# Conformer layer on one core: 56 of the 69 chunk transposes as DMA transposes

## The chip, the cores and the metric

The kernel runs on one core of a Trainium2 chip. A core has five engines, each with its own instruction stream: TensorE (PE, with the weight loads shown as PEld), VectorE (DVE), ScalarE (ACT), GpSimd (POOL) and SyncE (SP, which only issues DMAs here). The metric is device time of one execution in microseconds (us). Of three runs of the kernel before, the median is 881.56 us (881.25 to 883.18).

## The reference

Two sequences of 4000 tokens with 144 features in bf16 pass one conformer layer: half a feed-forward block, attention with 4 heads of 36, a gated convolution block, half a feed-forward block, and a layernorm. Each block works on a layernorm of x.

```python
h = _layernorm(x);  x = x + 0.5 * (_silu(h @ w_ff1a) @ w_ff1b)          # 144 -> 576 -> 144
h = _layernorm(x);  q, k, v = split(h @ w_qkv)                          # 4 heads of 36
att = softmax(q @ k.T * 36 ** -0.5) @ v;  x = x + att @ w_o             # 4000 x 4000 a head
h = _layernorm(x) @ w_pw1;  h = h[..., :144] * _sigmoid(h[..., 144:])
c = sum(hp[:, i:i + T, :] * dw[i] for i in range(5));  x = x + _silu(c) @ w_pw2
h = _layernorm(x);  x = x + 0.5 * (_silu(h @ w_ff2a) @ w_ff2b)
return _layernorm(x)
```

## The kernel before

**Tiles.** The tokens are cut into 16 chunks of 500 (`NCH`, 8 per sequence), and a chunk into 4 blocks of 125 tokens, which lie on the partitions; token p of a chunk's 500 is on partition p // 4. x stays in SBUF (`X`). A matmul wants the features on the partitions, so each layernorm output (`XN`, tokens on partitions) is transposed into `XT` (a chunk's 500 tokens in two parts, features 0 to 127 and the 16 that are left, padded to 80 rows) or, for q, k and v, into `XTQ` (two parts of 72 features). The attention output `AN` is transposed into `XT` in the same way, for W_o. That makes chunk transposes of four kinds in the middle of the kernel, 69 in all: 13 into `XTQ` and 56 into `XT`, 15 of these from `AN`. The first three chunks and the end of the kernel (`calm`, L975) transpose on PE.

**One chunk transpose** (`transp`, L1038, and `transp_q`, L1017, both by `blocks`, L994) goes through HBM. DVE transposes blocks of 32 x 32 words of four bytes in place, so two blocks of tokens are kept interleaved in pairs of bf16 (`XNI`, `ANI`, `XTJ`, `XTF` are views of that layout). SP then issues four DMAs that write the result into rows of a DRAM tensor (`rows`, `DR`), waits until they land, and issues two that read it back, transposed as a whole, into `XT` or `XTQ`. The matmuls that read `XT` (`xt`, L981) then step over the partner's elements, so their moving operand has a step of two elements. `XT`'s second part is zeroed once per slot by POOL (L1044), since the read fills only 16 of its 80 rows. `AN` is zeroed as a whole by POOL (L931, 128 x 2560) before its first use. There are 5 slots of `XN`, 5 of `XT` and 4 of `AN`.

**Layernorm** (`ln`, L1068): DVE makes the statistics, POOL the power -0.5 and the scaled row (`XN`), for chunks in the middle.

**Attention.** For each of 16 query chunks there are 63 tiles of keys of 64. PE makes the scores of a tile (two banks of PSUM), ACT the exponential (128 x 1000), and PE multiplies by v. Of these tiles 190 take another way: DVE makes the exponential by bit operations (`dve_tile`, L1770, five instructions each). All other blocks are woven in between: the front makes q, k and v of the 8 chunks of the first sequence; then attention runs over the query chunks, and the second sequence's first blocks, the convolution and the second feed-forward follow beside it.

**What sets the order.** The kernel is written as generators; a planner (`Sched`, L488, `pick`, L1899) gives each instruction a cost and a time and so makes a first order per engine. `Rec.op` (L177) records every instruction with what it reads and writes; all instructions are issued from one line, L398, which is therefore the line of nearly everything in the profile. Then `Rec.reorder` (L279) moves blocks of each engine's list by the letters of a table (`ORDER`, L38; P is "stay"), and `PLACES` (L111) gives the PSUM bank of each tile. Both tables were found by a search. `Rec.finish` (L344) puts the semaphore waits. The loads of x for the second sequence are issued by SP after a set number of chunk transposes (`later`, L860, in `blocks`).

The write and the read of one transpose, from `blocks`:

```python
op("dve", "transpose", v, v, r=[key], w=[key], cost=c_dve(320))
...
for a in range(4):
    args = "sp", "dma_start", DR[z, :, :, a, :, :].rearrange("k r g n -> r g k n"), v[32 * a:32 * a + 32, :, :, :]
...
for dst, f0, f1, n, cost, lat in reads:
    args = "sp", "dma_start", dst, d[f0:f1, :, :, :].rearrange("f g a n -> f g (a n)")[:, :, 0:n]
```

Of the kernel before, what the change touches and what calls it, by code (L numbers as in the profile page):

```python
# [8 lines left out]
F32 = mybir.dt.float32  # L9
# [30 lines left out]
        "PPPPPPQOQOPPPPPRPNPPQQQQLPPQORPNPRPTMORNNVO~OLNOMrMMNPMMNNNOMNNNOPLMQMMMNNPMMNSMNLMMOOPNSOMQMSPNOPU["  # L40
        "OMNRMOPPQIRMSNPNePNOOOcNNNNNNNNNOOLbNLOOQNSH]MMOLOMPMMOOOVPNOOOOPPPTOOOTPMUQMSLNNQQNQOQQNPPPPPTPPROK"
        "PPPPPPPPPPPP`PPPQKVPPKPPMPPRPUPPPROQQQRZOQQQRRKQRRSJPRRRRRRRWSZRNYUR~NHQ@R[KEGOOOPPPPKQOPPSPPSLPQMTP"
        "PPLQQQMPPPQVPPQOX_PTOPPCRTQQRGSQIQQSQRNV8OOQNNVSNOOLOPUUNN_MMWLNNRMMMMOOOPPPPPPQQNPPRSNRSSSORRVTR[OR"
        "AKQ@PPLOOQQNPPPPPUOOOOOPQOPPPPPUOOOOQRPLU`NNNXMMPNLQMNLZRNL`MN_YLLMK`KMNLILNQJMOOOPNYOPNOOOQNNZ^NNNN"
        "OOPNQNQOYP]CNNNNOMPMSO[NKOOQNVMPMMN`NbYMMMMNOMNIcLLNL[MMMNNQNRMJQLLROQSPLRNOQOPUQOMPQMPPRPVPLQOMQNPQ"
        "QQQSKPQSQKQQQQJPPPPPWQQSPKKQQUPPPSWPQRPQAVPPPQCVPQRPWHSYPHSOPQYPQEPQCPRZUPPSOOHDPR^OKOOOOPNOOOO^NOQN"
        "NOOOSNNNNS[NNNdRMNRKYNJWJNNNNNNGOOPP^YNNNNOMNNNNRNNPPPVROOLOOPPRZNNOOOOOPNOSOPNRPSMOOPQOQWNRPRLLNSZP"
        "NPQOIOQOTPPPRPQ]P^USPMMQIQKQQ8QTQQGMRRTQQKRRRRGLRSOMRPQQQJQQRPVP[OOOQEROO^IOQLNOOPPTTOMNQ[FOQNPPSPPM"
        "HPQOQQUPLOPNVPNOOSQNLUOOPNOXPPPLTQNLMPPPQOPPTOOPTPLOOQRNOPPPQOVPNOOOORZOP[PPMOOFRZOL[ROQKQTUBOKNFPPP"
        "_OOOOOOPNOOOOWNNVNNXMNTKMNOMZQOSLNOMSPSLLTPMOOUOPNOOTQOMOPPPQOPPPQOPPPTTQOSQSSSSNEEPQOPTPTMOMORSNNOP"  # L50
        "ROYPQOPQ^NPNPQOPAOOOOOSOOOPPPQQNPPPPPPXOOOOOOOaNPPPLOOOPUMOOOO[IOOPSOOQNPHPSWOOPPPPQGPPPPQQQMPPQQNPQ"
        "O_OOOPZOOOPI_NNNNZOPEOQWP^HKPHSJOLNOO`VPMRJOM^J`MPNKUNLUGNLJQNRIOPPRXOMOOOOPXMOPPMOOOPWOOPPPTKNOOPPP"
        "PPPPPPPQRPSYSQNQYZPRRRADIOXQGVOPJOORPIPPRRSSMR]MHOOQQQVRKNHPLPPPPPPPPPPRZQSQRRbHSGNQGPPQRRGLPQKQQQQJ"
        "QOQRPMQOPPQOSQNRMTROTNPXQQQEPJOQNPRPN_OPPPLRSOPLPPPGPPPSeOMPPQRJZPKLNNNN`NOKOVJNNNNcM`LMMMNNN]MNL]LL"
        "LLLLTWLXKMMVNQ_LMOPPQQ>MOOOTOMRbMMOOOOOTOOOQZIOPJMOOcOMPPT[PRORPEVHOPYCJQOQQGMOQQNQWNQNPPLSP_OaOOOPN"
        "PDPPPLOHPPQLPPPPQOTPNWNPPPWJNPPP`OIOPPPPPPPUQOELRP^TTQOZUPPCGOPQDJPPPPPPRPQWPRURPMFQQ_RPXDPQJLPNOJPN"
        "PPPPPSPPQ`PPTQQRERPQIQTNDPTPPJOPQQNPPUOPPSLPMPPRPQQRPJP[RNQQLaRJQSS[IQMGQQRPCZJPQOPQTPP@RPIPPPPQQQSS"
        "VXUQGNTQSSETDS`OQSCJQQdLOINQMRLLZMNSMMMMZLWPK]JMNLMTLNNNNVN`NNNNNROOPPJQOPLRPRMOQQRPLPXQQQRPTUQHFPQJ"
        "PPPPPPSPROUSPPTLPUOCOPNQOPROTWPRWRPVRZOY^YEOOPPMQ:;QDQQQQQQQQQEQQQMQOROVSMOTTQLVHROTRGNTVPHRPTRaJSQE"
        "QRSKNRNOQOPWQO=OOPNYOOOQNNOO]QOL_PNRO^NOUIPNK_MMW>MMMZMMMM]MMQLMMSNNOMOPPSOVNNPNXNPQOKQOQLQQQQUPPPHO"  # L60
        "QORPQMQOPQQSQOUVWNWMNOKOAOQOPPPPZWNNNOOLNNR^MNVNOMNNNNPSMN]NTNNNNNaNNNOQLN[RNOMRNHMSOSNPQGPQOPRXRPQW"
        "KOHOPPQYPPZPQRCO[I^NORFNNIZMMMNOWLNNNQMNRORRO_KPNOOOYNNNNNNOU^NSUHNKOJNOSOOQRJUPROTYMHNNURNNTMIPNQOU"
        "OOV[MNLNNNPYTNeJLNORNNGOO[]NNNNIQLMRLNRWOPUOO]OM`QO;LSOLO]JOJPRLLMRUNZMOVR[NPDOT^OOOFOSTOMNOSbPQLPRS"
        "_MORR_NPP^OHCNNNOZOWL~NHLMMNNNSOOXNOQQNSSOIVKPNPN]NOOOOOPPVOOOITNPPLPPQOWPPMRPNTKOOTNOPUMOOOQN`OOOPN"
        "OOPPPLOZOQQMPIQO^YROQQRLENO_PNPPPTQNNOROOSVO]QMNRNOPWTNOMNSOPQXbOOOQ[NO~NCdIMMMMMMMfbKMMMQMMJLMPLMUM"
        "MMNL^TR^JSLJQJUKPNLHQMPP`UNNNNOMOOOOPNOOPPPPQQNPQQQMUQQMSOPTQOPTPQUNQSPSQ<TRSSVEQQQHQQFPPPPPQSPMYTOL"
        "NNTMNNNP^[NOMNNQMMOLNN]PNOOR[OPKQN_ZLNESMOOKHOM[NPPLPNOOPPMQSTMNPQQQQRSQRRTCQVNGRNOMTTTMMNUPPQHNQSPM"
        "YVTQKLLSSOIJPSSPTMKORNOQOPPPPPPSORNSMRNRRRNQQRPFRPQQQQQQRPFQO"
# [14 lines left out]
    "dve": (
        "PPROQQQLPPPUUNNNNSMUNNPNOQOSPNSUMOPLOPTPNPNPPQQQQQQQQHPVPRPLPLPPPRSSNRNQVPUOODNUMPNPNPPQSPMXNOOQNNOO"
        "PPPPPPPSOOOPPQOPPPPPPPPPPPPPPPPQOQOPPPPPPROQQMQOQOPPQORSQMQQQQQRPQWQRPQLPQQQVQQQSUKTQ2KMPQQQRRORPQQR"
        "RRTQQRTTPP;RPQBPPSOOORPNSOPRPQKQOPPPPPPcPQcQQQQTPPERPDLDNRNRNQQQRFQNQQNQOPQOPPPQOPPPPPPPPPPPPPPPQQTM"
        "PPRPQQQQUQOQUQQQSQRVGPPPPSPPRPQQ/PQOPPSPPQQKPPPPPQOPPPPQOPPPPPROOPQQNROQNPPPPQOPQOQQNPPPQTQOPQRPSPRR"
        "NSPPRPQQQ;QOPPPPPPPPPPPROOQOPSOOOPQOROOUSUOOQSQHRGOPPPPROOPPQRPMQRNQNQOPPPPPPPPPPQOPRPRPQKQOPQQQRPQQ"
        "QQQWROOPQO?PPPPPPPPQOPSOPQePPROOPPEOPNOPNOOOOOQNPPPPPROOPPPPRPRRRRJQKPPQOPPPPPPPPPPPQOPPPYOOPNPRMSMR"
        "LQMPPQOPPPPPPPPPPPPPPPPPQOROOPROOPPPPPPPPQOPQOQOPPROOTOOOOQOSOOOPROQNPPPPPPPPPPPQSPPLQOPPPROOPPPPPPP"  # L90
        "PPPQOPPPPPPPPPPQOPPPPPQOPPPPPPPQQVPLTPMOLPPRPNPQOPPRRNNPROQNPPPPPPPPPPQOQOQORORNOPROOPPPQQNPPPPQOPQR"
        "NOPQOPPPPPSPNOQQNQOPQOPPPPPQQQMPPPPPPPQOPPPQOQRPMROQQMPPQOPSPNOPPUOOOOOWOOOOOOOPPQOPPQQQQRPRPQGPPPPP"
        "PPPPPPQOPPPPUOOOPNPQOSOOSNOSNZQMPLOPNOOOPPPPPPQQNQOQOPPPPQOQOPPPRUOUQOUIOJOOPPPQOPPPPUOOOOOPPPQOROQT"
        "QOPJQOPPPPPPPQQQMPQOPPQRNTNTNNNQNQOPQOROQNPPQOPPPPPPSPNOTOOOOPPPQOQQUPVQOTHPNIQOVOPPMPQMPTOPPRLTNOOO"
        "PPPPPPUOOOOOPQOPPSPSQSQSQUSTEOELQOPPPPPPPSOPNPPROOVOOPNOOPPROOVOOPNOOPQRPUQQQVRUQUPCKPDPPPPQOPPPPQOP"
        "QOQOSPNOhQOPPPPPHOPNOPPQOROQNGOOPPPQOQOPQOPRPNPPPPQOPPPPPROTPPLQRULVOUOJPNJPPQOQOPRPQMPPPPPPPPQQQQQK"
        "QRNRNORPNUOUP[LNKPMRNRNLNQSSMRMRPKQOQQNQOWPPMQOXOPRPNSOWNCPNORNRTTPJSQMSPPQRZOROQQQQTPUHOPRO4PPPPPPQ"
        "QQRLRPQLPPPPPPPPPQOQQQMPPPPPQQQMPPPPPPPPPQQQSLTRPSQJQQQQQRTOPPRPRSQSQRRTQUPQTDO/OPS]NSMOLNQQNLOVQUPU"
        "OKHPLRRNNPPPQOPQRPQQQQVQOPQORSOP?PPPPPPPPPPPPRORPQQRPWQQNPTPUPUKOO<OPQOROQQMPQOPQQNPQQSPTQNPHPPROOQS"
        "NPQULPNOORROQRPJPPSOOORO]SOSNPRWQQXPTRERGRRTTUXRTRSBSSSSSSSSAT@S&NNPPPPPPPPPPQO"  # L100
    ),
# [2004 lines left out]
```

## Time and profile before

| what | value |
|---|---|
| three runs: median (lowest to highest) | 881.56 us (881.25 to 883.18) |
| profiled execution: span from first to last instruction | 880.5 us |
| TensorE clock granted, mean | 0.998 |
| ACT, largest group: exponentials 128 x 1000 | 802, 749.3 us busy |
| DVE, largest group: PT from PS, 128 x 500 | 380, 250.1 us busy |
| DVE, chunk transposes (STREAM_TRANSPOSE) | 69, 34.5 us busy |
| POOL, XN rows 125 x 144 | 260, 150.4 us busy |
| POOL, memset of AN; memsets of XT | 1 of 2.23 us; 5 of 0.52 us |
| DMA queue q1 (SP's): packets, share of 16 engines | 112646, 13.8% |

The profiled execution has no time of its own besides its span; the median of the runs is 1.1 us above the span, and that is taken for what lies around it. Busy time of an engine is the union of its instructions' spans, and an instruction's span has a part that overlaps the next one, so a busy share near 100% can still hold small gaps. "Idle before" is the time an engine stood still ahead of a group, with what ended it. A row of the windows view gives the window, its length, then busy time and number of instructions for PE, PEld, DVE, ACT and POOL, then the granted clock, the DMA share and GB/s.

### The profile page before, as it was taken

Reading aid. Unit: us, or ns where it says so; the run is one execution under the profiler, and the core shown is the slowest. Engines: PE = TensorE matmul, PEld = TensorE weight load, DVE = VectorE, ACT = ScalarE, POOL = GpSimd, SP = SyncE. Lnnn points to the kernel's source line nnn. Section 1 sums busy time; section 2 is a strip of 40 time slices with the busy share of each in tenths; the row PEclk is TensorE's granted clock in tenths of the full one; section 3 lists DMA queues with packets and bytes.
Section 4 is the critical chain, followed back from the end, with each engine's and each line's share of the span. In section 5 each row is a group of like instructions: output and inputs, shape, how many; then the busy total and the mean of one; then the engine's idle time right before and its main releaser. Section 6 shows DMA issues by size and latency. Waiting matters only on the chain.

```text
span 880.5 us, 27000 instructions
## 1 busy us (share of the span) xinstructions
PE 851.5 (97%) x11419; PEld 380.2 (43%) x11419; DVE 822.7 (93%) x1812; ACT 849.6 (96%) x1098; POOL 300.4 (34%) x584
## 2 busy tenths in 40 slices
PE   8998999999999999999999999999999999999996
PEld 6543433344444443443444444344443433444366
DVE  7977999999999999999989999899999999999987
ACT  6799999999999999999999999999999999999986
POOL 7770331431336130252111813522513404032434
PEclk9999999999999999999999999999999999999999
DMA  3221001220221110212001120110110011001111
GB/s 100 44 55 38 16 18 36 62 51 16 40 49 38 23 38 22 45 24 45 16 9 30 36 44 23 23 26 20 43 31 18 21 37 20 17 12 36 27 27 33
DMA packets 114351, 28.80 MB, mean 33 GB/s; under 512 B 101090, under 2 KB 114230, under 8 KB 114230
## 3 DMA queue, kind: packets, MB, share of 16 engines
q1 hardware_dynamic: 112646, 26.39, 13.8%
q8 instruction: 89, 1.46, 0.7%
q10 hardware_dynamic: 1584, 0.69, 0.3%
q14 instruction: 32, 0.26, 0.1%
HBM read 13.44 MB, written 13.61 MB: 31 GB/s over the span
## 4 chain that ended last, share of the span: by engine, by line
ACT 46%; PE 33%; DVE 17%; POOL 2%; DMA 1%; issue 1%; SPq 1%; POOLq 0%; DVEq 0%
ACT PT L398 42%; PE PS L398 33%; DVE PT L398 7%; ACT TH L398 4%; DVE HT L398 2%; DVE ST L398 2%; DVE X L398 2%; DVE XN L398 2%; POOL RS L398 1%; POOL XN L398 1%; DVE KT L398 1%; DVE QT L398 1%; DVE AN L398 1%; SPq L398 1%; DMA rows<-XN 0%
## 5 line engine op out<-in xcount | busy, mean ns | idle before, releaser
L398 ACT ACTIVATE PT<-PS 128x1000 bf16<-128x1000 f32 (+1 forms) x818 | 757.2, 1074 | 4.1 <-PE PS L398 2.4
L398 PE MATMUL PS<-QT,KT 64*64 64x500 bf16 x3968 | 425.7, 385 | 13.0 <-ACT PT L398 5.2
L398 PE MATMUL PS<-PT,VA 64*37 64x500 bf16 x4728 | 411.5, 372 | 1.8 <-DVE QT L398 0.7
L398 DVE TENSOR_SCALAR PT<-PS 128x500 int16<-128x500 f32 x380 | 250.1, 668 | 5.8 <-PE PS L398 3.9
L398 PEld LDWEIGHTS PS<-QT,KT 64*64 64x64 bf16 x3968 | 123.4, 104 | 236.8 <-ACT PT L398 137.1
L398 POOL TENSOR_SCALAR RS<-ST 125x4 f32<-125x4 f32 x130 | 37.0, 284 | 482.2 <-DVE ST L398 475.6
L398 PEld LDWEIGHTS PS<-PT,VA 64*37 64x37 bf16 x4728 | 141.4, 96 | 96.2 <-DVE PT L398 18.7
L398 DVE TENSOR_SCALAR PT<-PT 128x1000 uint16<-128x1000 uint16 x380 | 154.5, 418 | 2.1 <-PE PS L398 0.8
L398 POOL TENSOR_SCALAR XN<-X,RS 125x144 bf16<-125x144 bf16 x260 | 150.4, 610 | 13.1 <-DMA out_dram<-XN 6.4
L398 DVE TENSOR_TENSOR PT<-PT 128x1000 bf16<-128x1000 bf16 x190 | 128.8, 679 | 1.3
L398 ACT ACTIVATE TH<-PS 128x500 bf16<-128x500 f32 (+3 forms) x194 | 107.3, 575 | 7.4 <-PE PS L398 6.5
L398 POOL TENSOR_TENSOR RS<-RS,NHALF 125x4 f32<-125x4 f32 (+1 forms) x93 | 91.7, 989 | 33.1 <-DVE RS L398 27.3
L398 DVE SCALAR_TENSOR_TENSOR HT<-TH,PS 128x500 bf16<-128x500 bf16 (+1 forms) x135 | 81.2, 615 | 12.8 <-ACT TH L398 12.0
L398 PE MATMUL PS<-XT,WA 80*128 80x500 bf16 (+5 forms) x288 | 74.5, 365 | 2.2 <-DMA XT<-rows 0.9
L398 DVE BATCH_NORM_STATS2 ST<-X 125x6 f32<-125x288 bf16 x160 | 65.7, 447 | 2.8 <-DMA X<-in_x_dram 2.7
L398 DVE SCALAR_TENSOR_TENSOR X<-PS,X 125x288 bf16<-125x288 f32 (+1 forms) x128 | 56.6, 449 | 6.5 <-PE PS L398 5.2
L398 PE MATMUL PS<-WB,HT 128*125 128x144 bf16 (+1 forms) x640 | 52.4, 230 | 0.7 <-ACT HT L398 0.5
L398 PEld LDWEIGHTS PS<-WB,HT 128*125 128x125 bf16 (+1 forms) x640 | 44.3, 136 | 14.5 <-issue 3.8
L398 PEld LDWEIGHTS PS<-XT,WA 128*128 128x128 bf16 (+1 forms) x288 | 21.2, 97 | 38.8 <-issue 10.6
L398 PE MATMUL PS<-U,DG 128*128 128x250 bf16 (+6 forms) x204 | 29.6, 264 | 0.0
L398 DVE STREAM_TRANSPOSE XN<-XN 128x320 f32<-128x320 f32 x54 | 27.0, 500 | 1.0 <-POOL XN L398 1.0
L398 POOL COPY U<-U 128x2 bf16<-128x2 bf16 (+1 forms) x54 | 9.2, 209 | 46.3 <-DVE U L398 46.3
(95 smaller groups left out, 522.6 us busy)
## 6 DMA issues: line engine op xcount, KB each, us to landing
rows<-XN SPq DMA_DIRECT2D x216, 40.0 KB, 2.0
XT<-rows SPq DMA_DIRECT2D x56, 128.0 KB, 2.0
rows<-AN SPq DMA_DIRECT2D x60, 40.0 KB, 2.0
X<-in_x_dram SPq DMA_DIRECT2D x15, 140.6 KB
XTQ<-rows SPq DMA_DIRECT2D x26, 70.3 KB
out_dram<-XN SPq DMA_DIRECT2D x13, 140.6 KB
XT<-rows SPq DMA_DIRECT2D x56, 16.0 KB, 1.9
out_dram<-XN SPq DMA_DIRECT2D x3, 70.3 KB
```

Of the source, the lines that this page charges most:

```text
L398: ins = getattr(eng, o.name)(*o.a, **o.k)
```

## The change

- The 56 chunk transposes into `XT` no longer go through DVE and HBM. For each of a chunk's four blocks SP issues one DMA transpose from SBUF to SBUF: 128 partitions x 256 columns of `XN` or `AN` (144 features of the block and 112 columns behind it) into 128 partitions x 2 x 128 of `XT`. Per chunk that is 4 DMAs in place of 4 writes and 2 reads, and no DVE instruction. In all 224 transposes take the place of 224 writes and 112 reads.
- `XN` (for these chunks) and `AN` are written block after block, no longer in interleaved pairs, and `XT` is read in steps of one element. Slots of `XN` and `AN` grow from 640 to 688 columns, since the last block's 256 columns reach past its 144.
- The five POOL memsets of `XT` go, since all its rows are now written. POOL's memset of `AN` becomes a memset on DVE (128 x 1376 words), placed in the front between those of `VL` and `VA`.
- The 13 transposes into `XTQ` stay as they are.
- In the planner "ghost" instructions keep the places, costs and latencies of what was taken out; they are dropped, and their dependencies passed on, at the start of `reorder`. `ORDER` and `PLACES` are both new tables. PE and ACT have the same instructions as before, in another order.

```diff
 ORDER = {
...
 PLACES = (
...
     def reorder(self, table):
+        real = {}
+
+        def through(o):
...
+        for o in self.ops:
+            if any(d.ghost for d, raw in o.deps):
+                o.deps = through(o)
+        self.ops = [o for o in self.ops if not o.ghost]
...
+    RW = 3 * D + 256
...
-    XNS = sb("XN", [NXN, 640])
+    XNS = sb("XN", [NXN, RW])
...
-    ANS = sb("AN", [NAN, 640])
+    ANS = sb("AN", [NAN, RW])
...
         op("dve", "memset", VL[:, :, :], 0.0, w=["VLZ"], cost=0.15)
+        side(None, "dve", "memset", ANS[:, :, :], 0.0, w=[("AN", a) for a in range(NAN)])
...
     def setup_dw():
-        op("pool", "memset", ANS[:, :, :], 0.0, w=[("AN", a) for a in range(NAN)], cost=2.2)
+        op("pool", "ghost", w=[("AN", a) for a in range(NAN)], cost=2.2)
...
     def xt(s, k, i0, i1=None, rows=TB):
         if i1 is None:
-            return XTJ[0:KK[k], s, k, i0 // 2, 0:rows, i0 % 2] if x_inter[s] else XT[0:KK[k], s, k, i0, 0:rows]
-        if x_inter[s]:
-            return XTJ[0:KK[k], s, k, i0 // 2:i1 // 2, 0:rows, :].rearrange("p g n j -> p g j n")
+            return XT[0:KK[k], s, k, i0, 0:rows]
         return XT[0:KK[k], s, k, i0:i1, 0:rows].rearrange("p (g j) n -> p g j n", j=2)
...
-            op("pool", "memset", XT[0:LP, s, 1, :, :], 0.0, w=wk, cost=0.5)
+            op("pool", "ghost", w=wk, cost=0.5)
         if dma:
-            yield from blocks((ANF if an else XNF)[:, u, :], key, s,
-                              [(XTF[0:128, s, 0, :, :], 0, 128, 128, 0.43, T_LAT), (XTF[0:16, s, 1, :, :], 128, D, 128, 0.43, T_LAT)], f"t{s}", wk)
+            yield need("dve")
+            op("dve", "ghost", r=[key], w=[key], cost=c_dve(320))
+            yield need("sp")
+            first = None
+            for i in range(NB):
+                args = "sp", "dma_start_transpose", XT[:, s, :, i, :], (ANS if an else XNS)[:, u, i * D:i * D + 256]
+                if first is None:
+                    first = op(*args, q=f"t{s}", r=[key], w=[("DT", s)] + wk, cost=W_COST, lat=W_LAT)
+                else:
+                    R.more(first, [key], [("DT", s)] + wk, *args, q=f"t{s}", cost=W_COST, lat=W_LAT)
+            yield need("sp")
+            first = op("sp", "ghost", q=f"g{s}", r=[("DT", s)], w=wk, cost=0.43, lat=T_LAT)
...
-    def ln(c, bs, e=False, inter=False):
+    def ln(c, bs, e=False, inter=False, pairs=False):
...
-            if inter:
-                dst = ANI[0:TB, a, :, zz * HD:(zz + 1) * HD, :].rearrange("p g (h d) j -> p g j h d", h=2)
-            else:
-                dst = AN[0:TB, a, :, zz * HD:(zz + 1) * HD].rearrange("p (g j) (h d) -> p g j h d", g=2, h=2)
+            dst = AN[0:TB, a, :, zz * HD:(zz + 1) * HD].rearrange("p (g j) (h d) -> p g j h d", g=2, h=2)
```

More of the change, by code (lines that the diff above doesn't have):

```diff
@@ L65 @@
[L65 to L68, printed above, removed]
+        "PPPPPPPPQOPPPPPQQNPQQSQOKPQQNUO^OPLZLeOLLULxLNIvJHMRMKLLLMPLLOSPNJTJXKLSPKKRUFKHKMNROJRPRPLWPNPPMmOT"
@@ L145 @@
 class Op:
-    __slots__ = ("eng", "name", "a", "k", "idx", "deps", "clock", "inc", "waits", "cnt", "q", "done", "t0", "t1", "kind", "step", "tile", "shared", "own", "acc", "base")
+    __slots__ = ("eng", "name", "a", "k", "idx", "deps", "clock", "inc", "waits", "cnt", "q", "done", "t0", "t1", "kind", "step", "tile", "shared", "own", "acc", "base", "ghost")
 class Place(int):
@@ L279, in reorder @@
     def reorder(self, table):
+        real = {}
+        def through(o):
+            if id(o) not in real:
+                ds = {}
+                for d, raw in o.deps:
+                    for x, how in through(d) if d.ghost else [(d, raw)]:
+                        if x is not o:
+                            ds[id(x)] = (x, how or ds.get(id(x), (x, None))[1])
+                real[id(o)] = list(ds.values())
+            return real[id(o)]
+        for o in self.ops:
+            if any(d.ghost for d, raw in o.deps):
+                o.deps = through(o)
+        self.ops = [o for o in self.ops if not o.ghost]
         lines = {}
@@ L1043, in transp @@
             xt_set.add(s)
-            op("pool", "memset", XT[0:LP, s, 1, :, :], 0.0, w=wk, cost=0.5)
+            op("pool", "ghost", w=wk, cost=0.5)
         if dma:
-            yield from blocks((ANF if an else XNF)[:, u, :], key, s,
-                              [(XTF[0:128, s, 0, :, :], 0, 128, 128, 0.43, T_LAT), (XTF[0:16, s, 1, :, :], 128, D, 128, 0.43, T_LAT)], f"t{s}", wk)
+            yield need("dve")
[10 more added lines that the diff above has]
+            first = op("sp", "ghost", q=f"g{s}", r=[("DT", s)], w=wk, cost=0.43, lat=T_LAT)
+            R.more(first, [("DT", s)], wk, "sp", "ghost", q=f"g{s}", cost=0.43, lat=T_LAT)
+            more_x()
             return
@@ L1133, in ln_trq @@
         inter = len(bs) == NB and not calm(c)
-        u = yield from ln(c, bs, inter=inter)
+        u = yield from ln(c, bs, inter=inter, pairs=inter)
         yield from transp_q(u, c, bs, inter)
@@ L1139, in parts, with side @@
         return [range(0, 2), range(2, 4)] if calm(c) else [range(0, 4)]
+    def side(like, *a, **k):
+        kept = dict(R.free), R.kind, R.last, R.filling
+        R.filling = True
+        o = op(*a, cost=0.0, **k)
+        R.free, R.kind, R.last, R.filling = kept
+        if like is not None:
+            o.done = like.done
+        return o
     def residual(c, g, mm, scale, rk, e=False):
```

177 lines of the change are left out of this document (87 added, 90 removed).

## The prediction

> **What bounds the kernel now.** I read the page first: the busy shares, then the chain of work that ended last.
>
> ```profile
> PE 851.5 (97%) x11419; PEld 380.2 (43%) x11419; DVE 822.7 (93%) x1812; ACT 849.6 (96%) x1098; POOL 300.4 (34%) x584
> ...
> ACT 46%; PE 33%; DVE 17%; POOL 2%; DMA 1%; issue 1%; SPq 1%; POOLq 0%; DVEq 0%
> ```
>
> The reader is to see three nearly full engines and a chain that passes between them. The change takes work from the third (DVE) and a little from PE, none from ACT. So I next cut the span into its stages.
>
> ```profile
> 0.00:22.00 22.00, 18.47 (x221) 15.09 (x225) 15.90 (x63) 13.93 (x30) 15.66 (x43) 1.00 0.40 100
> 22.00:44.00 22.00, 20.03 (x207) 11.67 (x207) 21.02 (x55) 16.15 (x30) 16.89 (x34) 1.00 0.21 44
> ...
> 88.00:264.00 176.00, 173.29 (x2374) 72.43 (x2372) 172.03 (x374) 174.26 (x209) 54.78 (x98) 1.00 0.17 36
> 264.00:572.00 308.00, 303.63 (x4110) 128.42 (x4108) 287.90 (x603) 306.01 (x382) 105.19 (x209) 1.00 0.14 30
> 572.00:836.00 264.00, 256.90 (x3538) 108.09 (x3534) 256.48 (x538) 263.72 (x324) 76.00 (x141) 1.00 0.12 25
> ```
>
> After the window and its length come PE, PEld, DVE, ACT and POOL. From 572 to 836 us ACT is busy 263.7 of 264. Busy time hides small gaps, because one exponential of 1000 columns is listed with 1082 ns but a row of 30 of them on the chain takes 26.51 us, 0.884 each. Worked out from the starts in the trace, the 802 exponentials follow one another by 0.908 on the mean, so 20 us lie between them. The same sum over all of ACT's instructions gives what ACT loses by stage: 14 us before 88, 16.6 from 88 to 572, 4.6 from 572 to 836, 7.7 behind it. A feeder that gets faster can win back the second figure at most, and hardly any of the third. From 88 to 264 DVE is as full as ACT (172.0 and 174.3 of 176).
>
> **What one chunk transpose costs today.** From the groups with shapes kept apart, the SP queue's timeline and the DMA issues:
>
> ```profile
> L398 DVE STREAM_TRANSPOSE XN<-XN 128x320 f32<-128x320 f32 x54 | 27.0, 500 | 1.0 <-POOL XN L398 1.0
> L398 DVE STREAM_TRANSPOSE AN<-AN 128x320 f32<-128x320 f32 x15 | 7.5, 499 | 0.0
> L398 PE MATMUL PS<-XT,WA 128*128 128x500 bf16 x112 | 44.2, 395 | 2.0 <-DMA XT<-rows 0.9 <-ACT PT L398 0.9
> L398 PE MATMUL PS<-XTQ,WQ 72*128 72x500 bf16 x60 | 17.9, 379 | 0.1
> ```
> ```profile
> 404.82 2.59 SPq L398 DMA_DIRECT2D rows<-XN  x4
> 408.82 0.81 SPq L398 DMA_DIRECT2D XT<-rows  x2
> ```
> ```profile
> rows<-XN SPq DMA_DIRECT2D x216, 40.0 KB, 2.0
> ```
>
> The DVE transpose is 0.50 us, four writes are issued in 2.6 us, SP waits until they land, then issues two reads; each lands 2.0 us after its issue. From the first write to the second read is 4.4 us (median of the 56). Ahead of it the DVE transpose stands in DVE's queue: its start is 1.5 us (median) behind the end of the last POOL instruction that wrote XN. So XT lands 1.5 + 0.4 + 4.4 + 2.0 = **8.3 us** after its source. How much later could it be? From the second read's issue plus 2.0, compared with the weight load that waited for that slot, the 56 uses had 2.2 us to spare (median), 9 less than 1, 23 less than 2, 41 less than 4. An XT later by 0.5 us would make PE wait 1.0 us in all, by 2 us 20, by 3 us 49.
>
> **The change, part by part.**
>
> DVE loses 56 transposes: 56 x 0.50 = 28 us busy, 24 us of its time by 0.43 from start to start. On the chain between 88 and 836 us I find twelve pieces of 0.41 to 0.51 us that are such transposes; 56 of 69 of them go, so ten, **-4.3 us**. The rest loosens DVE where PE waits for it, and the next chain is nearly as tight as this one; I let these two cancel.
>
> PE reads XT in steps of one element and no longer two. An XT matmul of 500 columns is listed with 395 or 388 ns, an XTQ one, read in steps of one, with 379: 13 ns on 284 instructions, 3.7 us. PE has a third of the chain: **-1.2 us**. The multiset of instructions on PE and ACT is the same in both listings.
>
> SP and the DMA engines: 224 transposes take the place of 336 transfers. No transpose DMA is in the trace. The cheapest issue there is 0.33 us, the longest 1.72; landings are 1.8 to 3.6. Four in a row would land 3 x 0.33 + 1.8 = 2.8 us to 3 x 1.72 + 3.6 = 8.8 us after the source, 5.5 earlier to 0.5 later than now. The nearest row is the write of rows (0.615, from SBUF, short pieces); one transpose has two blocks of 128x128, so I take two of these, 1.23 us, and land at 3 x 1.23 + 2.0 = 5.7 us, 2.6 earlier. SP is then held 4.9 us per chunk, as now (404.82 to 409.63), and what stands behind it on SP (loads of x, writes of the XTQ rows, stores) is no later. Since PE's order is fixed, an early XT gains only the waits: PE stood 0.9 us for XT near 70 us, and a little in the front; **-1.0 us**. Between a chunk's last f32 transpose and its first W_o matmul PE has 184 instructions in the old listing and 194 in the new (medians of the 16 chunks), so the new order doesn't lean on earlier landings.
>
> Here two pages of the Trainium skill differ. "VectorE: DVE Perf Modes", The three transpose paths, gives the crossbar DMA 1309 ns for 128x128 and VectorE 311 ns; two blocks in line would be an estimate of 2.6 us per instruction, which is the first rival below. "Advanced Engine Details and Errata", X-Bar Transpose (TRN2), says that transposing DMAs are as fast as plain ones; by that the sum stays as it is. No run so far shows either.
>
> POOL loses five memsets of XT (0.52 each) and the one of AN (2.23). Between 16.6 and 30.8 us POOL runs without a gap and makes the first three XN of the front, with two of the XT memsets between them; the second comes 0.5 earlier, the third 1.0. Its readers wait for other things too: **-0.5 us**.
>
> DVE gets the memset of AN, 1376 words. Memsets of 128 and 256 words took 165 and 272 ns, 0.84 ns a word, so 1.2 us. In DVE's order it stands behind the memset of VL. There DVE was idle 0.83 us, and 1.07 more before 11.0 us, waiting for x and PE. Cover for nearly all of it: **+0.2 us**, 1.2 if x comes sooner.
>
> Order and banks: both tables are new, 5076 lines of PE's listing differ. I can't price it from rows. At best ACT gets all its 16.6 us back, at worst all eleven stretches of 44 us run as the worst one did, which lost 2.4 us: 11 x 2.4 - 16.6 = +10. I take 0 and keep both ends.
>
> Sum: -4.3 - 1.2 - 1.0 - 0.5 + 0.2 = -6.8. The profiled execution's span is 880.5; 873.7 after. The median of the runs is 881.56, so 1.1 us lie around the span: **874.8 us**.
>
> **Rivals.**
>
> *The transposes hold the queue.* SP issues in order, and the four transposes of a chunk follow each other there. From 3 I + 2.0 = 8.3, that is I = 2.1 us for one, XT lands later than today, and PE, also in order, stands at its first XT weight load with the scores of attention behind it; ACT then has at most the tile in hand, 0.88 us. At 2.6 us a piece the last lands 4 x 2.6 = 10.4 after the source, 2.1 late: 22 us of PE waits over some 23 uses. I let half pass ACT's cover: 11 - 6.8 = +4, **886 us**; at 3 us a piece 3.7 late, 74 us of waits, 911. Against it: the longest issue seen is 1.72, and 8.3 us is a lot of room. For it: no row of this kind. Chance 0.15.
>
> *DVE was not the bound.* ACT's work is unchanged and carries 46% of the chain; the chain moves from the ten transposes to exponentials that ended just as late, and the PE savings end in waits for ACT. From 572 on ACT shows that such a state exists. **881 us**. Against it: 88 to 264, where DVE PT takes most of the chain near 150 to 220 us. Chance 0.10.
>
> *The new order is worse.* Same pieces, but PE waits longer for PT in the middle: up to +10, less the gains above, **883 us**. Chance 0.10; there is no row for or against.
>
> **How the numbers follow.** The forecast has 0.65. About 0.2% (1.8 us) is what a measurement of this kernel can tell from no change: faster 0.65, same 0.10 (second rival), slower 0.25 (first and third). Within the forecast the order's upper bound reaches 864; I give 0.07 to below 867. Upward the range must take in the third rival and the first at 2.6 us; 888 leaves out about 0.07 above. Range 867 to 888.
>
> **What would show it.** Right: DVE busy about 796 us; XT matmuls of 500 columns at about 379; no XT memset on POOL; issues of transposes below 2.1 us, landing near 2 us; PE waits for XT below 1 us in all; ACT's loss from 88 to 572 some 6 us smaller. Wrong: rows "PE waits for DMA XT" of tens of us and SP's timeline filled with transposes (first rival); DVE 26 us lighter with the exponentials still 0.908 apart (second); fewer DVE waits but more PE waits for ACT PT (third). The forecast falls if one transpose holds SP for over 2.1 us.

## The result, and the profile after

Over 22 runs the changed kernel's median is **886.33 us** (880.92 to 890.97), beside 882.01 (880.83 to 883.19) of 22 runs of the kernel before. The ratio is **1.0041, 95% interval 1.0030 to 1.0052**: slower by 0.4%, where I forecast 874.8. The spread is new too: 10 us, where before had 2.4. The profiled execution took 884.59 us, its span is 882.8.

The page of the changed kernel: the busy shares, and by engine the chain that ended last.

```profile
PE 845.1 (96%) x11419; PEld 384.6 (44%) x11419; DVE 805.2 (91%) x1757; ACT 848.8 (96%) x1098; POOL 287.8 (33%) x578
...
ACT 54%; PE 26%; DVE 9%; SPq 4%; POOL 3%; DMA 2%; issue 1%; POOLq 0%; DVEq 0%
```

DVE's share of the chain has halved, as meant, but SP's queue has come in with 4%. By stage (window, length, then PE, PEld, DVE, ACT, POOL):

```profile
0.00:22.00 22.00, 17.04 (x209) 13.93 (x209) 16.27 (x63) 13.14 (x29) 14.37 (x41) 1.00 0.41 100
...
88.00:264.00 176.00, 173.02 (x2406) 72.46 (x2405) 168.65 (x364) 174.11 (x210) 52.90 (x100) 1.00 0.15 30
264.00:572.00 308.00, 299.25 (x4076) 130.59 (x4080) 279.68 (x579) 303.96 (x382) 101.66 (x203) 1.00 0.13 26
...
836.00:882.80 46.80, 36.78 (x433) 27.27 (x432) 34.99 (x117) 32.54 (x72) 16.22 (x31) 0.96 0.14 34
```

From 88 to 264 us DVE is 3.4 us lighter and ACT does no more work for it (174.1, was 174.3). From 264 to 572 ACT does 2 us less. The tail is 2.3 us longer than the 44.5 us that were left behind 836 us before.

The best single view is a comparison of progress: the start of the k-th of the 818 exponentials on ACT in both traces, after minus before. It is -3.5 us at 200 us, -2.1 at 290, -1.1 at 320, stays within 0.8 us of that up to the last one (844 us, -1.1), and at the end of the span it is +2.3. So the change gained 3.5 us in the first quarter, lost 2.3 again between 220 and 320, and lost 3.4 behind the last exponential. In both places PE stands still for XT (weights and matmuls that read it wait for the DMA). PE's timeline, two stretches of the changed kernel:

```profile
269.27 0.60 PE L414 MATMUL PS<-XT,WP 128*128 128x500 bf16 x2 [2.36 <-DMA XT<-XN]
```
```profile
853.57 0.60 PE L414 MATMUL PS<-XT,WA 128*128 128x500 bf16 x2 [2.81 <-DMA XT<-XN]
```

and SP's timeline ahead of the first, with the end of the same stretch in the chain view (start, length, what):

```profile
254.68 5.89 SPq L414 DMA_TRANSPOSE XT<-AN  x4
260.62 5.11 SPq L414 DMA_TRANSPOSE XT<-XN  x4
```
```profile
263.19 1.25 SPq L414
264.44 0.04 issue
264.48 4.74 DMA XT<-XN
269.22 0.05 issue
269.27 0.61 PE PS L414 x2
```

XN was ready at 250.3 us, but its four transposes stand behind four others. The last is issued at 264.48 and takes 4.74 us to land; PE has stood since 266.91. In the tail the group is issued at 845.5, right behind its source, and its last one lands 4.2 us after its issue. In the list of DMA issues the median landing is 2.4 us; over the 56 groups the last of four lands 2.4 us after its issue in the median, a tenth take 3.7 or more, and **from the first issue until all has landed it is 7.0 us** in the median (6.2 to 8.6). The waits view (total, number, longest) of before and of the changed kernel: PE's matmuls wait for XT 6.3 us in four places (34, 244, 267 and 851 us), 0.9 in one before.

```profile
PE PS L398 <- DMA XT<-rows: 0.9, 1, 0.9
```
```profile
PE PS L414 <- DMA XT<-XN: 6.3, 4, 2.8
```

The same view has the other half of the answer, where DVE's freed time went, before and in the changed kernel:

```profile
DVE X L398 <- PE PS L398: 5.2, 12, 1.3
...
DVE PT L398 <- PE PS L398: 4.6, 12, 0.8
```
```profile
DVE PT L414 <- PE PS L414: 13.1, 35, 0.8
...
DVE X L414 <- PE PS L414: 10.3, 22, 2.3
```

Of the time taken from DVE, 13.6 us came back as waits for PE in these two rows.

### The profile page after: what moved, and what is told of

It is laid out like the page before. It is cut to its first block, busy times and chain, and to the rows that moved or that the text cites. A ratio compares the mean times of both kernels' runs of the same rounds, so it can differ in the third digit from the quotient of the medians.

```text
span 882.8 us, 26870 instructions
## 1 busy us (share of the span) xinstructions
PE 845.1 (96%) x11419; PEld 384.6 (44%) x11419; DVE 805.2 (91%) x1757; ACT 848.8 (96%) x1098; POOL 287.8 (33%) x578
## 4 chain that ended last, share of the span: by engine, by line
ACT 54%; PE 26%; DVE 9%; SPq 4%; POOL 3%; DMA 2%; issue 1%; POOLq 0%; DVEq 0%
ACT PT L414 49%; PE PS L414 26%; ACT TH L414 5%; SPq L414 4%; DVE PT L414 4%; DMA XT<-XN 2%; DVE ST L414 1%; POOL RS L414 1%; POOL XN L414 1%; DVE X L414 1%; DVE XN L414 1%; DVE HT L414 0%; DMA X<-in_x_dram 0%; DVE QT L414 0%; DMA out_dram<-XN 0%
## 5 line engine op out<-in xcount | busy, mean ns | idle before, releaser
L414 PE MATMUL PS<-PT,VA 64*37 64x500 bf16 x4728 | 405.0, 372 | 0.3 <-DVE QT L414 0.2
L414 POOL TENSOR_SCALAR RS<-ST 125x4 f32<-125x4 f32 x130 | 38.9, 299 | 450.4 <-DVE ST L414 443.7
L414 PEld LDWEIGHTS PS<-PT,VA 64*37 64x37 bf16 x4728 | 143.3, 96 | 92.4 <-issue 12.6
L414 POOL TENSOR_SCALAR XN<-X,RS 125x144 bf16<-125x144 bf16 x260 | 138.8, 550 | 26.6 <-DMA out_dram<-XN 20.1
L414 PE MATMUL PS<-XT,WA 128*128 128x500 bf16 (+4 forms) x288 | 73.2, 356 | 5.5 <-DMA XT<-XN 4.0
L414 PEld LDWEIGHTS PS<-WB,HT 128*125 128x125 bf16 (+1 forms) x640 | 44.6, 136 | 15.7 <-issue 4.9
L414 POOL COPY U<-U 128x2 bf16<-128x2 bf16 (+1 forms) x54 | 11.5, 247 | 76.1 <-DVE U L414 76.1
L414 PE MATMUL PS<-U,DG 128*128 128x250 bf16 (+7 forms) x204 | 29.3, 264 | 0.3
L414 PE MATMUL PS<-IDF,QT 128*125 128x128 f32 x128 | 23.1, 303 | 0.2 <-DVE QT L414 0.2
```

What stands on the lines that cost most here:

```text
L414: ins = getattr(eng, o.name)(*o.a, **o.k)
```

## The experiments

Two theories at first: the new order costs (A), or the DMA transposes do (B), with a third that DVE was not the bound (C). e1 to e4 ran on one chip, e5 to e8 on a second, e9 to e12 on a third, e13 and e14 on a fourth, each time with before in the same rounds; before's medians were 881.35, 881.46, 881.57 and 881.67. Ratios are to these.

| kernel | median us (lowest to highest) | ratio, 95% |
|---|---|---|
| e1 transposes, old order | 880.95 (879.77 to 882.96) | 0.9997 (0.9988 to 1.0006) |
| e2 before without the DVE transposes | 878.93 (878.74 to 879.88) | 0.9973 (0.9964 to 0.9983) |
| e3 changed, plain copies | 879.65 (879.38 to 879.85) | 0.9981 (0.9972 to 0.9990) |
| e4 changed | 881.96 (880.39 to 883.92) | 1.0011 (1.0003 to 1.0020) |
| e5 e1, memset on POOL | 880.25 (879.59 to 881.01) | 0.9986 (0.9977 to 0.9995) |
| e6 changed, memset on POOL | 882.64 (879.78 to 886.41) | 1.0013 (0.9999 to 1.0027) |
| e7 before, XT in steps of 1 | 880.94 (880.48 to 881.58) | 0.9993 (0.9984 to 1.0002) |
| e8 changed, last group twice | 892.26 (890.69 to 894.59) | 1.0124 (1.0106 to 1.0142) |
| e9 changed, two groups swapped | 884.50 (880.43 to 891.21) | 1.0034 (1.0016 to 1.0053) |
| e10 changed, mended | 880.10 (878.81 to 884.94) | 0.9997 (0.9983 to 1.0011) |
| **e11** e5, mended | **879.06** (878.42 to 880.17) | **0.9973 (0.9963 to 0.9982)** |
| e12 changed | 885.40 (881.19 to 890.06) | 1.0040 (1.0020 to 1.0059) |
| e13 changed, waits filled | 884.69 (883.05 to 887.03) | 1.0036 (1.0024 to 1.0048) |
| e14 changed | 884.68 (881.27 to 886.58) | 1.0033 (1.0023 to 1.0043) |

**e1, the transposes in the old order.** `ORDER` and `PLACES` of before; the ghosts stay in the lists until the table has been applied:

```diff
-        self.ops = [o for o in self.ops if not o.ghost]
         lines = {}
...
-            lines[e] = [o for blk in at for o in blk]
+            lines[e] = [o for blk in at for o in blk if not o.ghost]
+        self.ops = [o for o in self.ops if not o.ghost]
```

> The changed kernel with its DMA transposes, its VectorE memset and its layouts, but in the order and with the banks of the kernel before (every matmul, ScalarE and VectorE instruction stands where it stood; only the 56 DVE transposes are gone, and each group of four DMA transposes stands on SP where the four writes of rows stood). Theory A, the new order is what costs: the terms of the sum are right and this kernel takes 873 to 878 us, faster than both, with a spread from run to run as small as that of the kernel before (2.4 us). Theory B, the DMA transposes cost: they hold SP or land late, and this kernel takes 884 us or more, with runs spread over 8 us or more like those of the changed kernel. Theory C, DVE was not the bound: 880 to 883 us here, and the 28 us taken from DVE come back as waits of DVE for PE.

No gain, and a spread of 3.2 us. The time lies in theory C's range, and part of C's sign is there: the two DVE rows shown above are 9.3 and 5.9 us here. Theory B's 884 us did not come, and the profile has no wait of PE's matmuls for XT. It has one for XTQ, which was 0.9 us before:

```profile
PE PS L414 <- DMA XTQ<-rows: 2.0, 1, 2.0
```

Its first exponential is 1.6 us late, which it has won back only at 540 us, and the cause stands in the front (the stretch ahead of attention). PE's timeline, and the windows behind it (the granted clock is the third number from the right):

```profile
13.63 0.41 PE L414 MATMUL PS<-IDENT,XN 125*72 125x125 bf16 x4 [1.23 <-DVE XN L414]
```
```profile
14.00:16.00 2.00, 1.64 (x21) 1.28 (x19) 2.00 (x12) 1.32 (x4) 1.90 (x3) 0.93 0.37 100
16.00:18.00 2.00, 2.00 (x14) 1.56 (x13) 1.76 (x5) 1.41 (x5) 1.84 (x5) 0.50 0.33 86
```

PE stood 1.23 us for DVE, and from 15.7 us ran 3.4 us at half the clock.

**e2, before without the DVE transposes.**

```diff
-        op("dve", "transpose", v, v, r=[key], w=[key], cost=c_dve(320))
+        if q[:2] == "tq":
+            op("dve", "transpose", v, v, r=[key], w=[key], cost=c_dve(320))
+        else:
+            op("dve", "ghost", r=[key], w=[key], cost=c_dve(320))
```

> The kernel before without its 56 DVE transposes of the XT groups: rows are written from XN and AN as they are, so that XT holds other values and the result is not the reference's; everything else, the way over DRAM included, stays. It prices the first term alone. My sum gave the 28 us of DVE time 4.3 us on the path: 877 to 878 us. Theory C (DVE was not the bound): 880.5 us or more, within 0.2% of before.

-2.4 us, between the 4.3 of my sum and nothing. The progress comparison shows where: -1.3 by 83 us, -1.9 by 200, -2.4 by 560, nothing more behind it.

**e3, plain copies in the new order.**

```diff
-                args = "sp", "dma_start_transpose", XT[:, s, :, i, :], (ANS if an else XNS)[:, u, i * D:i * D + 256]
+                args = "sp", "dma_start", XT[:, s, :, i, :], (ANS if an else XNS)[:, u, i * D:i * D + 256].rearrange("p (k n) -> p k n", k=2)
```

> The changed kernel with each DMA transpose replaced by a plain DMA copy of the same 128x256 elements to the same place, in the same order: XT is not transposed and the result is not the reference's. If the transposing DMA is what costs (SP held 1.25 us for each, landing 2.4 us, long transfers beside the others), this kernel is faster than the changed one by 3 us or more and its runs are spread less. If the order costs, it stays at 884 to 888 us with the spread of the changed kernel.

Faster than the changed kernel beside it by 2.3 us, and its eleven runs lie within 0.5 us. A copy holds SP for 0.62 us (median) and lands in 2.0; from first issue until all has landed it is 4.1 us in the median (4.0 to 5.4). PE's matmuls wait for no XT, only for XTQ, 0.3 us. SP's timeline for the same two groups, and the row of the DMA issues (number, KB, median landing), with that of the changed kernel beside it:

```profile
254.00 2.71 SPq L414 DMA_DIRECT2D XT<-AN  x4
256.75 2.96 SPq L414 DMA_DIRECT2D XT<-XN  x4
```
```profile
XT<-XN SPq DMA_DIRECT2D x164, 64.0 KB, 2.0
```
```profile
XT<-XN SPq DMA_TRANSPOSE x164, 2.4
```

So with XT in time the new order is faster than before, and theory A in its plain form falls. e3 is 0.7 us above e2; that is order, memset, steps of one and the shorter way of XT together, so the order alone has no price from it.

**e4, the changed kernel again.**

> The changed kernel as it is, once more, as the measure for the other three on this chip: 881 to 891 us, median near 886. If the spread comes from the granted clock, the times fall with it from 0.999 to 0.993 as in the runs shown (nearly 2 us for each thousandth); if it is a place in the schedule that falls late in some executions, the profile of a slow execution shows waits for XT of 5 us or more beyond those of the first profile.

On this chip it is only 0.1% slower than before and spread over 3.5 us. Its profile has the waits of the first one, shorter: 1.79 us at 267 and 0.84 at 850, where the last group now lands 2.35 us after its last issue, and not 4.2. Its progress against e3's shows what the transposes cost and where, since order, layouts and chip are the same: e4 is 0.1 us behind up to 240 us, 0.6 at 255, 1.8 from 270 to 320, 1.5 from 400 to the last exponential and 2.1 at the end. It falls back only where its matmuls wait for XT, 0.3 us at 244, 1.8 at 267 and 0.8 at 850. The first profile of the changed kernel, not taken beside e3, has the same steps against it, larger: 0.1, 0.7, 2.5, 2.2 and 4.8.

**e5 and e6, the long memset back on POOL**, in e1 and in the changed kernel:

```diff
-        side(None, "dve", "memset", ANS[:, :, :], 0.0, w=[("AN", a) for a in range(NAN)])
...
-        op("pool", "ghost", w=[("AN", a) for a in range(NAN)], cost=2.2)
+        op("pool", "memset", ANS[:, :, :], 0.0, w=[("AN", a) for a in range(NAN)], cost=2.2)
```

> e1 (DMA transposes in the order and with the banks of the kernel before) with the long memset of AN back on POOL, where the kernel before has it. e1's profile has PE idle for 1.23 us at 12.4 us, a half granted clock from 15.7 to 19.1 us and its first exponential 1.6 us later than before; e2, which has the old front, has none of these. Theory memset: the DVE memset in the front delays PE by about 1 us and at times brings the half clock; without it the gap at 12.4 us is gone, the time is 878.5 to 879.3 us like e2's 878.9, and the runs lie within 1.5 us. Rival, the DMA transposes: 880 us or more, still spread over 3 us.

> The changed kernel with the long memset of AN on POOL again (its new order and the DMA transposes stay). If the memset in the front is what makes the time of the changed kernel vary, its gap of PE at 11.2 us goes, the spread shrinks to below 2 us and the median falls by 1 us or more against the changed kernel's 882.0 of e4. If the waits for XT in the new order (at 267 and 851 us) are what costs and varies, median and spread stay as in e4.

In the old order it helps: PE's gap at 12 us shrinks from 1.23 to 0.40 us, and the runs lie within 1.4 us. The median is 1.2 us below before, where e1's was 0.4 below, and not the 2 to 3 us that the theory asked for. What is still missing against e2 is mostly a wait of 1.8 us for XTQ at 70.5 us (e11), which e2 doesn't have. In the new order the gap goes as well (0.7 us won by 83 us), but neither median nor spread falls (882.64 and 6.6 us, on another chip than e4): there the memset is not what varies.

**e7, steps of one.** In `xt` of before, only the last line is left of each case, so that the interleaved `XT` is read straight.

> The kernel before with XT read in steps of 1 where it was read in steps of 2 (the interleaved data stay, so that the result is not the reference's). It prices the second term alone: my sum gave it 1.2 us, so 880.1 to 880.4 us beside 881.4 of before. If PE's 3.7 us lie beside ScalarE's work: within 0.4 us of before.

0.5 us, which the interval doesn't tell from nothing. Its profile, the longest of its eleven runs, shows where a gain can have gone: progress is -1.8 us at 200 us, and back at -0.6 by 540. Between them PE's matmuls wait for XT at 245, 393 and 528 us, 1.6 us in all, where before has none of these three: the faster PE seems to run into the old way over HBM.

**e8, the last group twice.** After `reorder` the last four transposes get a twin ahead of them, and wait for it:

```diff
+    at = [i for i, o in enumerate(R.ops) if o.name == "dma_start_transpose"][-4:]
...
+    R.ops[at[0]].deps = R.ops[at[0]].deps + [(o, True) for o in new]
+    R.ops[at[0]:at[0]] = new
```

> The changed kernel with the last group of four DMA transposes (issued at 845 us) issued twice, the second time after the first has landed, so that this XT lands about 7.5 us later (5.1 us of SP and 2.4 us of landing). The matmul at 853 us then waits some 8 to 11 us instead of 0.8 to 2.8. If the wait alone costs, the time grows by at most 7.5 us. Theory clock: a wait of PE of some us halves the granted clock for one or more windows of 3.4 us (as in e1's front), so the profile shows a clock of 0.5 behind 853 us beside the one at the very end, and the time grows by more than the wait. Should the tail not be on the path (something else late there), it grows by less than 4 us.

PE's wait at 852 us became 9.1 us, 6.3 to 8.4 more than in the four profiles of the changed kernel, and the median is 9.6 us above that of e6, which differs in the memset too. Windows of its profile:

```profile
852.00:862.00 10.00, 0.88 (x4) 0.36 (x3) 1.51 (x6) 0.59 (x1) 1.42 (x2) 0.70 0.17 34
862.00:876.00 14.00, 13.90 (x148) 11.95 (x147) 11.32 (x42) 8.39 (x22) 4.40 (x6) 0.85 0.03 7
```

The clock is halved from 856.0 to 866.2, that is for 5 us after XT has come. From the last exponential to the end of the span is 10.7 us longer than in e4, with a wait that is 8.3 us longer. So the tail's XT is on the path, and here the wait costs more than its length. In the same profile a window of half clock stands behind the 1.7 us wait at 267.

**e9 and e10, the places mended in the new order.** e9 swaps the two groups on SP; e10 does so too, has the memset on POOL, and moves the waiting matmuls of the tail behind the fourteen that follow:

```diff
+        sp = lines["sp"]
+        sp[148:156] = sp[152:156] + sp[148:152]
+        pe = lines["pe"]
+        pe[11155:11171] = pe[11157:11171] + pe[11155:11157]
```

> The changed kernel with one edit: on SP the group of four transposes from XN that stands behind the four from AN at 254.7 us goes ahead of them. Both groups are the same work; XN was ready at 250.3 us and its reader is first (PE waits for it at 267 us, 1.7 to 2.4 us in all four profiles of the changed order), while the reader of the AN group comes 2 us later. Theory queue: the wait at 267 us goes, and with it the half clock that e8 shows behind it in one execution: the median is 1 to 2 us below the changed kernel on this chip, and the spread is smaller by the 1.8 us that one half window took. Rival, the landing and not the queue (or the AN group then late instead): a wait of the same size at 267 to 270 us, the time as that of the changed kernel within 0.5 us.

> The changed kernel with three edits: the swap of e9, the long memset of AN back on POOL (e6), and in the tail the two matmuls that wait for the last DMA group (2.8 us in the first profile) moved behind the fourteen matmuls that follow them (1.1 us of PE). If the waits for XT at 267 and 851 us and the memset make the whole difference to e3 (879.65 us beside 881.35 of before), this takes 879 to 880 us, spread below 2 us. If the new order is slower for another reason, it stays above 881 us.

e9's profile shows the swap at work: no wait at 267, and progress at 299 us is -4.5 us, where e4 had -2.8. So the group ahead on the queue was needed for this wait; in the first profile so was the long landing, since with the median 2.4 us in place of 4.7 XT would have been there at 266.9, as PE came. But the median is only 0.9 below e12's, within what the spread allows: in the tail PE stands 2.7 us as before, with a half window behind it. In e10 eight of twelve runs take 878.8 to 880.3 us; the other four 883.4 to 884.9, at a granted clock of 0.994 or 0.995. The median comes near the 879 to 880 that was expected, the spread of 6.1 us does not, and the interval doesn't tell it from before. Its profile is one of these: a wait for XT of 2.3 us at 38.5 us, then 6.8 us at half the clock.

**e11, the old order mended.** One edit more to e5, on SP, at the group of 58 to 63 us:

```diff
+        sp = lines["sp"]
+        sp[57:62] = sp[58:62] + sp[57:58]
```

> e5 (DMA transposes, the order and banks of before, the memset on POOL) with one edit on SP: at 62.7 us the four writes of rows for XTQ go ahead of the fourth transpose of the group in front of them, so that XTQ lands about 1.3 us earlier; e5's PE waits 1.8 us for it at 70.5 us. If that wait is on the path: 0.8 to 1.3 us below e5, some 879.0 us against 881.4 of before, faster than both kernels by more than 0.2%. If not: as e5, 880.2 us.

As expected: the wait for XTQ is gone, 879.06 us. All that PE waits for XT in its profile:

```profile
PEld PS L416 <- DMA XT<-XN: 1.2, 1, 1.2
PE PS L416 <- DMA XT<-XN: 0.7, 1, 0.7
```

This version beats before by 0.27%, and the changed kernel beside it (e12) by 6.3 us.

**e12, the changed kernel a third time.**

> The changed kernel as it is, for e9 and e10 on the same chip: 880.4 us without a half window, 1.5 to 2 us more for each one; so a granted clock of 0.998 or 0.999 goes with times below 882.5 us, and 0.995 or less with times above 884 us.

This time the profile caught a long execution (888.14 us). Its windows at 34 and at 269 us:

```profile
34.00:37.00 3.00, 1.70 (x11) 0.71 (x12) 1.90 (x5) 1.06 (x2) 2.94 (x8) 0.94 0.30 64
37.00:40.10 3.10, 3.10 (x15) 1.97 (x14) 2.36 (x6) 1.62 (x5) 0.21 (x1) 0.51 0.23 46
...
269.40:272.20 2.80, 1.08 (x14) 0.75 (x18) 2.27 (x5) 1.75 (x3) 2.71 (x4) 0.99 0.00 0
272.20:275.60 3.40, 3.40 (x26) 1.41 (x30) 1.91 (x5) 2.31 (x4) 3.06 (x6) 0.51 0.00 0
```

PE stands 1.5 and 1.7 us for XT, and each time 3.4 us at half the clock follow; progress falls by 2.3 us against e4's at the first, by 0.3 at 247 us and by 1.4 at the second. My rule of the clock held for the slow end only: 884.33 us came at 0.998.

**e13 and e14, the waits filled.** Ahead of four waiting matmuls come matmuls that do nothing needed:

```diff
+    for like, n in [(pe[k], n) for k, n in ((313, 12), (361, 10), (3437, 24), (11155, 24))]:
...
+            o.eng, o.name, o.a, o.q, o.inc, o.cnt = "pe", "matmul", (PSV[:, bk, 0:128],), None, False, 0
+            o.k = dict(lhsT=IDENT[:, :], rhs=IDENT[:, :], start=True, stop=True)
```

> The changed kernel with 70 idle matmuls more (IDENT by IDENT, 0.056 us each, into the bank that the next matmul clears): 12 ahead of the matmul that waits for XT at 34 us, 10 at 39 us, 24 at 267 us and 24 at 851 us. The waits for XT stay as long as they are (a filler runs while PE would stand), but PE is busy for 0.6 to 1.3 us of them. Theory clock: the half windows of 3.4 us come because PE is busy for less than some 55% of one window, so nearly all of them go: granted clock 0.997 or more in nearly every run, times from 880 to 883 us, median 1.5 us or more below the changed kernel on this chip. Rival, the half windows and the long times come from something else that varies (late DMAs, the chip): the same spread up to 888 us or more.

> The changed kernel as it is, on the chip of e13 and in the same rounds: as on three chips before, a median of 882 to 886.5 us, single runs up to 884 to 891 us, with a granted clock down to 0.991 to 0.996.

The clock behaved as expected (0.997 or 0.998 in all six runs of e13), the time didn't: both medians are 884.7. On this chip e14 had few low clocks anyway (eleven of twelve at 0.996 or more), so the half clock can hardly be its main loss; that the waits alone are is not shown. In e13's profile PE stands or fills for 1.6 us each at 34 and 40 us, and is already 1.8 us behind e4 at 60. The test is not clean: in e13 the group issued at 33.9 us, which PE needs at 40, has a transpose that holds SP for 2.40 us, and in all four profiles of the changed kernel it has 1.24 to 1.26. So with the fillers other transposes were long, and the landings moved too. What e13 shows is that without low clocks the median stays as high; for the half clock as a cause the slow end is left. Over the 55 runs of the changed kernel the 32 at a clock of 0.997 or more have a median of 882.65 (880.4 to 888.4), the 14 at 0.995 and 0.996 885.7, the 9 below that 887.6 (886.2 to 891.0).

## Why the prediction was wrong

**The bound, and DVE's transposes (-4.3).** Sign right, size wrong: e2 measures -2.4. I counted ten pieces of the chain as gained and let the next chain cancel against what loosens elsewhere. It didn't cancel: in the changed kernel the exponentials are still 0.908 us apart (0.905 in e2), the second rival's sign, and DVE's time turned into waits for PE. So that rival had nearly half of it. The place was wrong as well: the ten pieces lie between 88 and 836 us, where e2 won 1.1 us; the other 1.3 it won ahead of 83 us, where the sum counted nothing. DVE's busy time fell by 17.3 us in e2, not 28, because it is a union of spans that overlap; the plain sum of DVE's instruction times fell by 25.7 (943.5 to 917.8).

**Steps of one (-1.2).** The matmuls got faster as forecast (383 and 377 ns, 379 forecast), but the time by 0.5 us at most (e7).

**XT earlier (-1.0).** This is the step that failed. The price of one transpose was good in the median: 1.25 us of SP (1.23 taken), far below the 2.1 at which I let the first rival begin. But four of them and their landing take 7.0 us, not 5.7: the landing is 2.4 us and not 2.0, and some transposes and landings are long. That alone left half of the 2.6 us that I counted as won. SP is held 5.5 us a group in the median (5.0 to 6.3) and not 4.9, so what stands behind is later: in the old order it was XTQ (e1 and e5; mended in e11).

From this I concluded that "an early XT gains only the waits", and from medians of 184 and 194 instructions that the new order doesn't lean on earlier landings. A median doesn't see the few tight places, and the count was of W_o's uses, whose XT comes from AN, while every wait in the changed kernel's traces is for an XT from XN. The new order does lean on early landings, at 34, 39, 244, 267 and 851 us. There a group waits behind another on SP, or starts with its source, and the plain copies' 4.1 us (e3) are in time where 6.2 to 8.7 are not.

The traces show it use by use, as the time from the landing of a group to the weight load that waits for it. With the same transposes the least of the 56 is 0.9 us in the old order (e1); in the new one seven have 0.1 us or less (first profile). With plain copies in the new order (e3) the least is 1.9, and five have 2.9 or less, which is what a group of transposes is later by (7.0 against 4.1).

In place of -1.0 it cost +2.3 us against copies that land in 4.1 us (e4 less e3, one chip), and 4.7 to 5.5 where the changed kernel stood 3.0 to 3.8 us above before (e14, e12) and e3's -1.7, from the other chip, is set against it. In the old order, with one swap on SP, the same transposes show no cost: e11 is as fast against its before (-2.5) as e2 with the way over DRAM (-2.4), on another chip and with steps of one besides. So the first rival had the right queue, but not its point of decision: the slack at each place decides, not the mean price of a transpose. It is also priced by another rule (4 I, 10.4 us at 2.6) than the one that lets it begin (3 I + 2.0, which gives 9.8); the forecast doesn't use it.

**Memsets (-0.5 and +0.2).** The DVE memset took 1.2 us as forecast. I said its cover was nearly whole. It was not: the idle 0.83 us ahead of VA's memset stands there again behind the new one (0.82 us in e1 and in the changed kernel), so this part covered nothing. Behind it PE waits, whose gap grew to 1.23 us in e1 (0.40 before). Against their befores e5 is 0.8 us better than e1, so moving the memset cost about that in the old order; that is across two chips.

**Order anew (0).** Close, as far as it can be had: e3 is 0.7 us above e2, and that includes the memset, steps of one and the earlier XT. What I did not see is that order and transposes can't be priced apart; the order decides which transposes are late.

**The sum** of what was measured on one chip: -2.4 (e2) + 0.7 (e3 less e2) + 2.3 (e4 less e3) = +0.6, which is e4; it closes by its construction and proves nothing by itself. **Around the span** lie 1.8 us and not 1.1 (884.59 beside 882.8), too little to matter. **The range** held 886.33 by luck: its top was drawn for the first rival, with 22 us of waits over some 23 uses; what came was 6.3 us in four, at half the price of a transpose. **What would show it**: the XT matmuls and the absent memsets came as said; DVE at 805 in place of 796, and PE's waits for XT at 6.3 us in place of below 1, were the signs of the two steps that failed. ACT's loss between 88 and 572 us was to be some 6 us smaller; summed over the distances from one ACT instruction to the next, less the median of its kind, it is 15.9 us in both traces.

**Open:** why the changed kernel's median differs by 4 us between chips while before's differ by 0.7. Landings and half windows vary from run to run, but no run separates the chips. Why some transposes and landings are long is open as well.

## What to carry to other kernels

Price a moved transfer at its tightest uses and not at its mean: list for each consumer how long it can still wait, and look for two groups in a row on one queue. An order found by a search can lean on early landings at a few places; test a new way of transfer in the old order too, where here it was worth 0.27% with two small edits. On a kernel with a full TensorE, a spread that appears with a change is itself a finding: look for the waits of PE and at the granted clock behind them.

## What the runs showed of the hardware

**A short wait can halve the clock for 3.4 us.** The granted clock switches in steps of 3.413 us. In e1, e8, e9, e10 and e12 windows at 0.5 stand behind waits of PE of 1.2 to 2.7 us (the tail of e8: 9.1), while the first profile had 2.8 us without one. If a grid of that step is laid through each trace's switching points, PE was busy for half of the window or less in eight windows, and seven times the next one was at half clock; at 54 to 58%, two of six; above, one (e10's second half window in a row, behind a window that was 88% busy at half clock). That would make it chance where the grid cuts a gap; the grid's place is inferred. The Trainium skill, "TensorE: Matmul & The Clock Gate", Part 1, gives the same 3413 ns for a free-running window and half the rate after one idle window. Its practical rule, no idle gaps of PE above about 3.4 us, is too mild here: gaps of 1.2 to 2.7 us were enough.

**Transposing DMAs vary.** Of the 224 in each profile 26 to 29 hold SP for 1.6 to 2.9 us, nearly all others 1.17 to 1.26; largely the same ones in each execution of one program (21 in all four profiles of the changed kernel, two of them in e13 too), and of the plain copies in e3 one. One such transpose can be followed to PE: it is the second of the first group, at 22 us, and PE's wait at 34 us is for the group behind it on SP. In the eight profiles that have transposes in the new order and no fillers it took 1.65 us with a wait of 0.46, 1.92 to 1.99 with 0.72 to 0.81, 2.24 with 1.05, 2.53 and 2.68 with 1.42 and 1.48. The last of a group lands 2.4 us after its issue in the median and up to 4.9; in the tail of the changed kernel 2.35 in two profiles and 4.1 or 4.2 in two, and PE's wait there is 0.7 or 0.8 us with the one and 2.8 with the other. The Trainium skill, "Advanced Engine Details and Errata", X-Bar Transpose (TRN2), says that transposing DMAs are as fast as regular ones. For single ones of 64 KB the measurement differs: here a transpose of 128x256 held SP for twice as long as the plain copy of the same shape (1.25 and 0.62 us) and landed 0.4 us later.
